# A fused attention and two-MLP kernel: the weights' buffers move 32 bytes within SBUF, the moving sides stay

## The chip, the core and the metric

The kernel runs on one core of one Trainium2 chip. The metric is the device time of one execution in microseconds (us); lower is better. A core has TensorE (PE; its weight loads are listed apart as PEld), VectorE (DVE), ScalarE (ACT), GpSimd (POOL) and SyncE (SP, which issues the DMAs here). SBUF is the on-chip memory of 128 partitions; a tile occupies the same bytes in each of them, so one byte address per partition says where a tile lies.

## The reference

Causal attention with 2 batches, 12 heads, 448 positions and head size 64 gives 896 tokens of 768 values. Two dense layers follow:

```python
x = attn_out.transpose(0, 2, 1, 3).reshape(B * S, H * D)   # 896 x 768
h = (x @ w1) * (x @ w2) @ w3                               # 768 -> 1024 -> 1024
x = h @ w_out                                              # 1024 -> 768
h = x @ w_in                                               # 768 -> 2048
g = h * np.clip(h + 3.0, 0.0, 6.0) / 6.0
out = g @ w_out2                                           # 2048 -> 768
```

## The kernel before

**Arithmetic.** Every dense product is made from two float32r parts of each operand, a high one and a low one, with three matmuls: high times high, high times low, low times high (the three `nc.tensor.matmul` in the `go` functions). Each matmul has its own load of 128 x 128 weights (LDWEIGHTS) and a moving side of 448 columns (one batch), or 384 columns for the product of weights.

**Stages.** Attention runs first (scores `s` L469, transposes `ptp` L517, values `o` L542), and beside it and after it the product of two weight matrices, `w_out` and `w3` (`pw`, L614). Then come the products with `w1` and `w2` (`pa`, L747), with the product of weights (`px`, L863), and with `w_in` and `w_out2` (`pg`, L747, and `po`, L928). `pa` and `pg` use seven products in place of eight (the function `multiply`; `side` names the seven). `Plan.issue` decides the order of all instructions on each engine beforehand, by ranks and by costs written as constants; no address enters it.

**Where the operands lie.** Pools are laid out one after the other. From low addresses: 1,152 bytes of other things, `consts` (pool `cp`), then pool `ws` with seven buffers of 8,192 bytes: three `raw` (where weights land from HBM: `vir`, `vor`, `w1r`, `wrr`, `wpr`, `w3r`) and four `hl` (the high and low parts that TensorE loads as weights: `w3`, `w2a` to `w2d`, `wp`, `vja`, `vjb`, `vo`). Then the empty tile `gap`, and pool `xp` with the attention output `xt`, later `x2t`. Further up lie `wr` (moving side of `pw`), `ab` and `g` (moving sides of `px` and `po`), and the tiles T1 to T4 (moving sides of `pa` and `pg`).

All steps inside these tiles from one operand of a matmul to the next (from the high part to the low one, from one block of 128 rows to the next, from batch to batch) are multiples of 256 bytes, as are the distances between buffers of one pool, modulo 256. So every dense matmul has one place modulo 256 bytes for its weights and one for its moving side. In the built program, before:

- `hl` weights start at 160 modulo 256 (25,760 is the first).
- Moving sides (`xt`, `x2t`, `T1` to `T4`, `wr`, `ab`, `g`) start at 224 modulo 256.
- Three of the seven products of `pg` (P6, P3 and P4 of `multiply`) take their weights from `xp` tiles (named `v` in the profile), from element 16 on (`ASIDE`, L46): 32 modulo 256.

Below, *the distance* is the start of the moving side minus the start of the weights, modulo 256: 64 for all `hl` weights, 192 for the weights `v`. Of the 2,256 dense matmuls, 384 (`pw`), 576 (`po`), 288 (`px`), 576 (`pa`) and 216 of the 432 of `pg` take `hl` weights; the other 216 take `v`.

The lines that hold these places:

```python
            s2, a22, s4 = ((own(i), ASIDE) for i in range(3))        # pg: weights in xp tiles
            s2, a22 = ((parts(f"{f[0]}{c}", f[1]), 0) for c in "cd") # pa: weights in hl buffers
```

Of the kernel before, what the change touches and what calls it, by code (L numbers as in the profile page):

```python
# [9 lines left out]
F32 = mybir.dt.float32  # L10
# [178 lines left out]
def attention_moe_moe2(ctx: ExitStack, tc, q, k, v, w1, w2, w3, w_out, v_in, v_out, out):  # L189
# [12 lines left out]
    P = 128  # L202
# [22 lines left out]
    cp = ctx.enter_context(tc.tile_pool(name="cp", bufs=1))  # L225
    ws = ctx.enter_context(tc.tile_pool(name="ws", bufs=2))

    gap = ctx.enter_context(tc.tile_pool(name="gap", bufs=1))
    gap.tile([P, 16], F32, name="gap")
    xp = ctx.enter_context(tc.tile_pool(name="xp", bufs=1))  # L230

    dp = ctx.enter_context(tc.tile_pool(name="dp", bufs=1, space=bass.MemoryType.DRAM))
    pd = ctx.enter_context(tc.tile_pool(name="pd", bufs=DENSE_BANKS, space=PSUM))
    consts = cp.tile([P, 8], F32, name="consts")
    three = consts[:, :1]

    ctx.enter_context(tc.manual_schedule())
# [769 lines left out]
```

## Time and profile before

| | before |
|---|---|
| time, median of 3 runs (lowest to highest) | 546.82 us (546.42 to 547.03) |
| time of the profiled execution | 546.7 us |
| its span, first to last instruction | 544.9 us |
| TensorE busy with matmuls | 538.9 us of 544.9 |
| VectorE, ScalarE, GpSimd busy | 72%, 55%, 21% of the span |
| granted TensorE clock, mean | 0.999 |

The span is what the trace covers; 1.8 us of the time lie around it. Busy time of TensorE counts each matmul from its start to its modelled end, and matmuls overlap; how fast TensorE goes is therefore read from the starts of matmuls that follow each other.

### The profile page before, as it was taken

What the parts mean: (1) busy time and instruction counts of PE and PEld (TensorE: products, weight loads), DVE (VectorE), ACT (ScalarE), POOL (GpSimd) and SP (SyncE); (2) the same over time, 40 slices, a digit from 0 to 9 for tenths busy, and PEclk for the clock granted to TensorE, in tenths of its full rate; (3) what the DMA queues carried; (4) which work ended last, traced back from release to release, by engine and by line L of the source; (5) the groups of instructions that cost most, each with busy time, mean ns of one, the idle gap of its engine ahead of it and who ended that gap; (6) DMA issues with size and microseconds to landing.
All of it is one profiled execution on the core that took longest, in us unless ns stands there. A gap on an engine that the chain in (4) does not pass through costs nothing.

```text
span 544.9 us, 8101 instructions
## 1 busy us (share of the span) xinstructions
PE 538.9 (99%) x2886; PEld 485.0 (89%) x2886; DVE 394.8 (72%) x746; ACT 298.2 (55%) x582; POOL 114.7 (21%) x150
## 2 busy tenths in 40 slices
PE   9999999999999999999999999999999999999997
PEld 7767677789999999999999999998999999999996
DVE  4888878777924798988728659998977876776322
ACT  4778777776525465544525336986656642653000
POOL 4778568571001111110000111010110101000000
PEclk9999999999999999999999999999999999999999
DMA  8687676436143333322513012538284647563664
GB/s 318 234 292 252 221 264 214 165 111 202 44 117 130 117 115 117 117 96 97 213 59 115 1 58 90 182 152 293 86 305 159 242 130 252 182 230 101 196 194 135
DMA packets 33224, 89.91 MB, mean 165 GB/s; under 512 B 3232, under 2 KB 21664, under 8 KB 30624
## 3 DMA queue, kind: packets, MB, share of 16 engines
q1 hardware_dynamic: 33184, 89.40, 48.2%
q8 instruction: 22, 0.36, 0.3%
q14 instruction: 18, 0.15, 0.1%
HBM read 75.24 MB, written 14.16 MB: 164 GB/s over the span
## 4 chain that ended last, share of the span: by engine, by line
PE 97%; DMA 1%; ACT 0%; DVE 0%; issue 0%; POOL 0%; SPq 0%; POOLq 0%; ACTq 0%
PE po L928 21%; PE pw L614 12%; PE paX L747 11%; PE px L863 11%; PE pgX L747 10%; PE s L469 7%; PE paZ L747 5%; PE pgZ L747 5%; PE o L542 5%; PE ptp L517 4%; PE paY L747 3%; PE pgY L747 2%; DMA vir<-in_moe_w_in 1%; PE warm L570 1%; PE warm L448 1%; DVE wr L305 0%
## 5 line engine op out<-in xcount | busy, mean ns | idle before, releaser
L928 PE MATMUL po<-g,vo 128*128 128x448 f32 x576 | 116.3, 362 | 0.0
L928 PEld LDWEIGHTS po<-g,vo 128*128 128x128 f32 x576 | 108.0, 187 | 7.2
L614 PE MATMUL pw<-wr,w 128*128 128x384 f32 x384 | 75.9, 347 | 0.3 <-DVE wr L305 0.3
L495 POOL TENSOR_SCALAR prb<-prb,sums 128x448 f32<-128x448 f32 (+6 forms) x84 | 65.5, 796 | 32.9 <-DVE sums L489 16.8
L614 PEld LDWEIGHTS pw<-wr,w 128*128 128x128 f32 x384 | 65.8, 188 | 2.2 <-issue 0.7
L863 PE MATMUL px<-ab,wp 128*128 128x448 f32 x288 | 57.9, 362 | 0.0
L863 PEld LDWEIGHTS px<-ab,wp 128*128 128x128 f32 x288 | 54.0, 187 | 3.6
L715 DVE TENSOR_TENSOR o<-po,o 128x448 f32<-128x448 f32 x36 | 22.4, 623 | 38.6 <-PE po L928 36.7
L469 PE MATMUL s<-ks,qs 128*128 128x448 f32 (+6 forms) x168 | 48.1, 392 | 0.0
L472 DVE CUSTOM_DVE_ANT_0 z<-s,maskb 128x448 f32<-128x448 f32 (+6 forms) x84 | 34.4, 420 | 18.4 <-PE s L469 9.4
L476 ACT ACTIVATE prb<-z,sums 128x448 f32<-128x448 f32 (+6 forms) x84 | 42.3, 508 | 4.7 <-DVE sums L472 4.7
L299 POOL TENSOR_SCALAR vja<-vir 128x768 fp32r<-128x768 f32 x8 | 7.6, 946 | 172.9 <-DVE x2t L697 70.4
L469 PEld LDWEIGHTS s<-ks,qs 128*128 128x128 f32 x168 | 27.3, 190 | 6.1 <-issue 0.9
L525 ACT COPY pt<-ptp 128x512 f32<-128x512 f32 (+1 forms) x48 | 24.8, 561 | 11.9 <-PE ptp L517 11.8
L517 PEld LDWEIGHTS ptp<-ident,prb 128*128 128x128 f32 x192 | 22.2, 139 | 5.7 <-issue 3.1
L542 PE MATMUL o<-pt,vr 128*64 128x448 f32 (+3 forms) x192 | 25.8, 393 | 0.0
L303 ACT CAST vo<-vor 128x1024 fp32r<-128x1024 f32 x12 | 13.6, 1132 | 21.6 <-PE po L928 18.1
L517 PE MATMUL ptp<-ident,prb 128*128 128x128 f32 x192 | 25.4, 272 | 0.0
L542 PEld LDWEIGHTS o<-pt,vr 128*64 128x64 f32 (+1 forms) x192 | 11.3, 135 | 15.2 <-issue 10.0
L708 DVE SCALAR_TENSOR_TENSOR g<-rab,g 128x448 fp32r<-128x448 f32 x32 | 20.6, 651 | 1.1 <-ACT g L706 1.1
L706 ACT ACTIVATE g<-rab 128x448 fp32r<-128x448 f32 x32 | 18.3, 578 | 4.7 <-DVE rab L704 4.7
L702 ACT ACTIVATE rab<-q,consts 128x448 f32<-128x448 f32 x24 | 16.0, 669 | 8.5 <-DVE q L892 8.1
(148 smaller groups left out, 1051.9 us busy)
## 6 DMA issues: line engine op xcount, KB each, us to landing
vor<-in_moe_w_out SPq DMA_DIRECT2D x12, 1024.0 KB, 6.5
w3r<-in_moe_w SPq DMA_DIRECT2D x8, 1024.0 KB, 5.1
sums_of<-o SPq DMA_DIRECT2D x36, 224.0 KB, 2.7
o<-sums_of SPq DMA_DIRECT2D x36, 224.0 KB, 2.7
wrr<-in_moe_w_out SPq DMA_DIRECT2D x8, 768.0 KB, 6.3
w1r<-in_moe_w SPq DMA_DIRECT2D x8, 768.0 KB, 5.4
w2r<-in_moe_w SPq DMA_DIRECT2D x8, 768.0 KB, 4.3
vjr<-in_moe_w_in SPq DMA_DIRECT2D x8, 768.0 KB, 4.7
```

The lines of the kernel that those rows point to most:

```text
L469: plan.op("pe", pe4(n), lambda: nc.tensor.matmul(ps[:, :n], qs[u][:, t].rearrange("p h i -> p (h i)"), ks[u][:, :n], start=True, stop=True ...
L472: plan.op("dve", dve(n) + 0.09, lambda: nc.vector.tensor_tensor_reduce(out=z[:, :n], in0=ps[:, :n], in1=maskb[:, S - n:], scale=-SCALE, sc ...
L476: plan.op("act", act(n, True) + 0.2, lambda: nc.scalar.activation(pb[:, OFF[t]:OFF[t] + n], z[:, :n], AF.Exp, bias=sm[:, 0, t:t + 1], scal ...
L495: nc.gpsimd.tensor_scalar(s, s, sm[:, 1, t:t + 1], 1.0, ALU.mult, ALU.mult)
L517: nc.tensor.transpose(ps[:w, i * P:(i + 1) * P], pb[:, OFF[t] + kb * P:OFF[t] + kb * P + w], ident)
L525: plan.op("act", act(cut), lambda: nc.scalar.copy(dst()[:, :cut], ps[:, :cut]), reads=[ps], writes=[d.at((g, 0))], rank=rank)
L542: nc.tensor.matmul(ps[T * j:T * j + T, kb * P:S], vr[u][:w, kb, j, :], d[:w, base[kb]:base[kb] + TQ - 2 * kb, j, :], start=kb == 0, stop=k ...
L614: nc.tensor.matmul(ps[:, :W], weight(n, a, kk), hls[m][:, c, at_:at_ + W], start=kk == 0 and a == c, stop=kk == KF - 1 and a == LO)
L715: plan.op("dve", dve(S), lambda: nc.vector.tensor_tensor(o[:, :], ps[:, :S], o[:, :], ALU.add), reads=[ps], writes=[o], rank=rank)
L747: nc.tensor.matmul(ps[:, :S], hl[:, a, off + kk * P:off + (kk + 1) * P], t[:, c], start=first and kk == 0 and a == c, stop=kk == HK - 1 an ...
L863: nc.tensor.matmul(ps[m, b][:, :S], weight(n, a, kk), ab[kk][:, c, cols(b)], start=kk == 0 and a == c, stop=kk == KF - 1 and a == LO)
L928: nc.tensor.matmul(ps[:, :S], hls[n][:, a, at_:at_ + P], gt[k][:, d, cols(b)], start=kk == 0 and a == d, stop=kk == KC - 1 and a == LO)
```

## The change

`consts` grows from 32 to 64 bytes and `gap` shrinks from 64 to 32. So the seven buffers of `ws` lie 32 bytes higher (1,184 becomes 1,216 for the first, 25,760 becomes 25,792 for the first `hl`), and every tile from `xp` on stays where it was (`xp` begins at 58,592 in both). `hl` weights now start at 192 modulo 256, and their distance to every moving side is 32 where it was 64. The weights `v` stay at distance 192. The instructions and their order are the same on all five engines; only addresses in `ws` differ.

```diff
     ws = ctx.enter_context(tc.tile_pool(name="ws", bufs=2))
 
     gap = ctx.enter_context(tc.tile_pool(name="gap", bufs=1))
-    gap.tile([P, 16], F32, name="gap")
+    gap.tile([P, 8], F32, name="gap")
     xp = ctx.enter_context(tc.tile_pool(name="xp", bufs=1))
...
-    consts = cp.tile([P, 8], F32, name="consts")
+    consts = cp.tile([P, 16], F32, name="consts")
     three = consts[:, :1]
```

## Rows read from the trace of the kernel before

**Rows 1.** The page, part 1: busy time, share and instructions by engine.
```profile
PE 538.9 (99%) x2886; PEld 485.0 (89%) x2886; DVE 394.8 (72%) x746; ACT 298.2 (55%) x582; POOL 114.7 (21%) x150
```
**Rows 2.** All waits of TensorE: total, times, longest in us.
```profile
PE warm L448 <- POOL ident masks.py:199: 1.4, 1, 1.4
PE pgZ L747 <- ACT q L889: 0.6, 1, 0.6
PE pw L614 <- DVE wr L305: 0.3, 1, 0.3
```
**Rows 3.** The chain that ended last: start, length in us, instructions in a row.
```profile
13.08 2.62 PE warm L570 x24
...
127.24 38.17 PE pw L614 x219
...
266.81 57.00 PE px L863 x285
```
**Rows 4.** The same chain over one part of `pg` and around it.
```profile
404.07 1.80 PE pgX L747 x9
405.87 1.81 PE pgY L747 x9
407.67 1.81 PE pgX L747 x9
409.49 1.80 PE pgZ L747 x9
411.29 1.80 PE pgX L747 x9
413.09 1.82 PE pgZ L747 x9
414.91 1.81 PE pgX L747 x9
416.73 9.60 PE po L928 x48
```
**Rows 5.** Timeline of TensorE there: start, length, operands; weights are the second name.
```profile
403.91 1.96 PE L747 MATMUL pgX<-x2t,vja 128*128 128x448 f32 x9
405.71 1.97 PE L747 MATMUL pgY<-x2t,vja 128*128 128x448 f32 x9
407.51 1.98 PE L747 MATMUL pgX<-T2g,v 128*128 128x448 f32 x9
409.33 1.96 PE L747 MATMUL pgZ<-T1g,vjb 128*128 128x448 f32 x9
411.13 1.97 PE L747 MATMUL pgX<-T3g,vjb 128*128 128x448 f32 x9
412.93 1.98 PE L747 MATMUL pgZ<-x2t,v 128*128 128x448 f32 x9
414.75 1.98 PE L747 MATMUL pgX<-T4g,v 128*128 128x448 f32 x9
416.57 0.96 PE L928 MATMUL po<-g,vo 128*128 128x448 f32 x4
```
**Rows 6.** Busy time by stretch: length, each engine's busy us (instructions), clock, DMA share, GB/s.
```profile
127.00:167.00 40.00, 40.00 (x232) 39.84 (x233) 25.07 (x39) 19.37 (x35) 3.15 (x3) 1.00 0.34 105
267.00:324.00 57.00, 57.00 (x287) 53.43 (x286) 32.80 (x50) 21.78 (x35) 2.42 (x3) 1.00 0.20 65
324.00:362.00 38.00, 38.00 (x191) 35.45 (x190) 35.83 (x57) 29.78 (x51) 4.09 (x5) 1.00 0.40 146
362.00:493.00 131.00, 130.45 (x651) 121.67 (x651) 105.18 (x155) 76.73 (x117) 9.41 (x9) 1.00 0.58 197
```
**Rows 7.** The chain around TensorE's one wait for data in `pg`.
```profile
372.45 7.04 DMA vir<-in_moe_w_in
...
379.57 0.93 ACT vir L323
380.50 0.42 ACT q L889
...
380.96 2.08 PE pgZ L747 x9
```

## The prediction, made before the changed kernel ran

> **What bounds the kernel now.** I read the busy shares first, then TensorE's waits, then the chain that ended last with the count of matmuls in each of its pieces. TensorE is busy 538.9 of 544.9 us [rows 1], and all its waits for other engines come to 1.4 + 0.6 + 0.3 = 2.3 us [rows 2]. So the time is the sum of the intervals between the starts of matmuls, and only what changes such an interval, or makes a wait longer, can change the time. The granted clock is 1.00 in the stretches shown, its 2.4 GHz level [rows 6].
>
> The interval itself: 285 matmuls of `px` in 57.00 us are 200.0 ns each, and 219 of `pw` in 38.17 us are 174.3 [rows 3]. `px` streams 448 columns, `pw` 384. At one column per clock these would be 186.7 and 160.0 ns, so each interval has some 13 to 14 ns on top, about the same for both lengths. It does not grow with the columns, so it goes with something that happens once in a matmul, and what does is the load of the next weights. That load runs while the matmul streams: two streams read SBUF at once, and the change shifts one against the other.
>
> Does their relative place cost anything? One part of `pg` has both sorts of weights side by side. With `hl` weights (distance 64) nine matmuls take 1.80 us from the first start to the next nine's: 403.91 to 405.71, 405.71 to 407.51, 409.33 to 411.13, 411.13 to 412.93. With the weights `v` (distance 192) they take 1.82: 407.51 to 409.33, 412.93 to 414.75, 414.75 to 416.57 [rows 5]. The chain gives the price with fewer rounding errors: from 404.07 to 416.73 us are 63 matmuls in 12.66 us [rows 4]; 36 of them at 200.0 ns are 7.20, which leaves 5.46 us for the 27 with `v`, 202.2 ns each. The pairs differ in nothing else that I find: same shape, same type, same tile T or `x2t` as moving side. So the distance, or the place of the weights, is worth 2.2 ns a matmul between 64 and 192. This is the one row on which the forecast rests.
>
> **The change part by part.** *Constants and gap.* Nothing is computed with the added bytes; 0 us. *The `raw` buffers.* DMAs write them 32 bytes higher, and ACT, DVE and POOL read them there. The trace has no transfer or instruction at another place, so nothing prices this directly. Below, a gain is bounded by the only wait that such work ends: 0.6 us before `pgZ`, behind a load of 7.04 us [rows 2, 7]. Above, VectorE in 324 to 362 us is busy 35.83 of 38.00 [rows 6]: it could slow by 2.17 us, 6%, before it fills this stretch. I take 0 for both, since TensorE is what covers them (busy 38.00 of 38.00 there), and keep a rival for the end above.
>
> *The `hl` weights.* The distance goes from 64 to 32 for 384 + 576 + 288 + 576 + 216 = 2,040 matmuls, 1,656 of them with 448 columns. The 216 with `v` stay as they are. No dense matmul of before has the distance 32; the nearest rows are 64 (200.0 ns) and 192 (202.2). From below: if 64 isn't the cheapest distance, I can bound the gain only by the whole excess, 13.3 ns x 2,040 = 27 us; a gain of the size of the one difference that the trace shows is 2.2 x 1,656 = 3.6 us. From above: one more excess of the same size, 13.3 x 2,040 = 27 us. There is also a row at distance 0, but in plain float32: the 24 `warm` transposes of 128 columns take `ident` for both sides, and 109 ns each [rows 3] are 0.85 ns a column, half the speed of `px`, with only 2.5 ns left over two clocks a column. At half the speed two streams in one place disturb each other little; at full speed no row tells.
>
> I take the price of the row with `v`, that is +2.2 ns, on the matmuls of 448 columns: 1,656 x 2.2 ns = 3.6 us. Why this and not 0: the interval demonstrably depends on where the two streams start, and a distance of 32 puts the weights' first reads nearer to the moving side's than in either row, so that keeping the cheaper of the two prices would be the luckier result. For `pw` (384 columns; no row at another distance) the bounds are 0 and 384 x 2.2 = 0.8 us; I take half, 0.4. Sum: 3.6 + 0.4 = +4.0 us on the profiled execution's 546.7, 550.7 us. That execution lies 0.1 us below the median of the runs, 546.82, so that the two bases agree.
>
> **The rivals.**
>
> *No change.* The two streams run at different speeds (weight loads are busy 53.43 of 57.00 us of `px` for 128 columns each, against 448 that move [rows 6]), so they drift past each other, and a shift of 32 bytes moves the meetings without changing their number; or weights and moving side don't meet at all, and the 13 ns belong to the swap of weights. For it: the excess is about the same in `pw` and `px` [rows 3], and the `warm` row shows two streams from one address at little cost. Against it: 202.2 beside 200.0 [rows 4]. Then every interval stays, 546.8 us. The Trainium skill, TensorE: Matmul & The Clock Gate, section Step-by-step: what each phase is for, states this as a rule: TensorE has two independent SBUF read ports, and loading the next weights doesn't steal read bandwidth from the running matmul. The Trainium skill, SBUF — State Buffer, section SBUF: two separate sides, agrees: only VectorE and GpSimd share a port. By that rule, address differences cost nothing and the time stays; the trace doesn't settle it, but 1.82 beside 1.80 us [rows 5] speaks against its strict form.
>
> *Faster.* 64 is not the cheapest distance, or a start of the weights at 192 modulo 256, a multiple of 64, lets a load touch one unit less than a start at 160 or 32, which are both 32 beyond such a multiple. For it: each start in the trace, of `hl`, of `v` and of the moving sides, is 32 beyond a multiple of 64, so no row excludes it. Against it: the one other distance is dearer. Sized by the same 2.2 ns, 1,656 + half of 384 matmuls give -4.0 us: 542.7 us.
>
> *A real collision.* With the streams 32 bytes apart the moving side stands still for about as long again as it does now: +13.3 ns x 2,040 = 27 us, 574 us; half of it gives 560. This decides from about +6 ns a matmul on. Against it: nothing in dense rows; the `warm` row shows none at half speed.
>
> *VectorE fills its stretch.* If reads and writes in the shifted buffers cost VectorE over 6% more, 324 to 362 us is bound by it: above 548 us. The trace shows nothing that would slow it.
>
> **How the numbers follow.** The forecast, +1.1 to +7 us, has 0.40; no change 0.29; faster 0.22; a collision of 7 us and more 0.08; VectorE 0.01. A difference of 0.2%, 1.1 us, is about what a measurement of this kernel can tell from no change. So slower has 0.49, same 0.29, faster 0.22. The range reaches down to a gain of 1.2 times the one sized above (542 us, some 0.08 below it) and up into the collision case (557 us, +4.6 ns a matmul, some 0.08 above it). The likeliest case alone spans 548 to 554 us.
>
> **What would show it.** The chain's piece of 285 `px` matmuls is the cleanest gauge: 57.0 us means no change, 57.6 the forecast (202.2 ns each), 56.4 the faster rival, above 58.5 a collision. The pieces with `v` should stay at 1.82 us in all cases; if they move too, the distance isn't what counts. `pw`'s 219 should go from 38.2 to between 38.2 and 38.7. VectorE's means should stay. The forecast is wrong if 32 bytes are below the grain at which the streams meet, or if the dearer price of `v` comes from where its high and low parts lie and not from the distance.

## The result and the profile after

The changed kernel takes 552.49 us in the median of 4 runs (552.24 to 553.25), beside 546.62 for the kernel before: a ratio of 1.0102, 95% interval 1.0083 to 1.0121. It is slower: the medians differ by 5.87 us, the spans of the two profiles (550.5 and 544.9 us) by 5.6. The profiled execution took 552.24 us.

One number from ahead of the prediction has to be put right first: `pa` and `pg` have 504 matmuls each, not 576 and 432, and of those of `pg` 288 take `hl` weights. The sums that the prediction uses (2,040 matmuls with `hl` weights, 1,656 of them with 448 columns, 216 with `v`) stand.

The page's busy times and all waits of TensorE, after (compare [rows 1, 2]):

```profile
PE 545.0 (99%) x2886; PEld 486.4 (88%) x2886; DVE 394.7 (72%) x746; ACT 298.9 (54%) x582; POOL 115.2 (21%) x150
```
```profile
PE warm L448 <- POOL ident masks.py:199: 1.4, 1, 1.4
PE pw L614 <- DVE wr L305: 0.3, 1, 0.3
```

TensorE is busy 6.1 us longer; VectorE, ScalarE and GpSimd are busy as long as before within 0.7 us. No wait came in, and the one of 0.6 us in `pg` is gone. So the loss is in the intervals of TensorE itself. The chain that ended last, after (start, length, instructions in a row; compare [rows 3]), and behind it the pieces of before that [rows 3] does not show:

```profile
128.22 38.16 PE pw L614 x219
...
271.15 58.90 PE px L863 x285
...
498.64 48.02 PE po L928 x240
```
```profile
165.41 1.80 PE paX L747 x9
...
323.81 1.80 PE pgX L747 x9
...
493.11 48.02 PE po L928 x240
```

`pw` with its 384 columns is as before (38.17). `px` takes 58.90 us for 285, 206.7 ns each, in place of 57.00, 200.0 ns each. But `po` takes 48.02 us for 240, 200.1 ns each, as before, with the same new distance of 32. So the distance alone doesn't set the interval. The place where it falls, in the chain of after at the start of `pg`:

```profile
330.05 1.86 PE pgX L747 x9
331.91 1.85 PE pgY L747 x9
333.76 1.21 PE pgX L747 x6
334.97 1.80 PE pgZ L747 x9
336.77 2.41 PE pgX L747 x12
...
341.58 1.82 PE pgZ L747 x9
```

And the timeline there, which names the weights:

```profile
329.88 2.02 PE L747 MATMUL pgX<-x2t,vja 128*128 128x448 f32 x9
331.75 2.02 PE L747 MATMUL pgY<-x2t,vja 128*128 128x448 f32 x9
333.60 1.37 PE L747 MATMUL pgX<-T2g,v 128*128 128x448 f32 x6
334.81 1.96 PE L747 MATMUL pgZ<-T1g,vjb 128*128 128x448 f32 x9
336.61 1.36 PE L747 MATMUL pgX<-x2t,vja 128*128 128x448 f32 x6
```

Twice nine matmuls with `vja` take 1.86 and 1.85 us (206 or 207 ns each by their starts, but for the last) up to the first piece with weights `v`, six matmuls at 333.6 us. Right behind these six, nine with `vjb`, whose distance is the same as that of `vja`, take 1.80 us, and no stretch with `hl` weights goes back to 1.86 for the rest of the kernel. From the end of `pw` (128.22 + 38.16 = 166.38, before 165.41) to the first matmul of `pg` (330.05, before 323.81) the changed kernel loses 163.67 - 158.40 = 5.27 us; 792 matmuls there at 6.67 ns each would be 5.28. Behind that, up to the last 240 of `po`, it is 0.71 us shorter than before (168.59 beside 169.30): the 18 slow matmuls at the start of `pg` cost 0.12 us, and the wait of 0.6 us is gone. The rest of the span's difference, 0.98 us ahead of `pw`, is scatter between executions as far as the profiles show: the six whose operands lie up to there as after the change start `pw`'s 219 anywhere from 127.52 to 128.62 us, and that of before with `ASIDE` 48 (below), whose `hl` weights lie as before, starts them at 128.46, beside 127.24.

The theory made of this, *the rhythm*: at distance 32 a row of matmuls can go on in either of two rhythms, 200.0 or 206.7 ns, and keeps the one that it is in. What came before decides; here the hand-over from `pw` brings the slow one, and the first weights at distance 192 end it. Its rivals: the operands of `pa` and `px` cost 206.7 ns and those of `pg` and `po` don't (*the stage*); or it is the place of the weights alone, a multiple of 64, and not the distance (*the place*).

### The profile page after: what moved, and what is told of

It is laid out like the page before. It is cut to its first block, busy times and chain, and to the rows that moved or that the text cites. A ratio compares the mean times of both kernels' runs of the same rounds, so it can differ in the third digit from the quotient of the medians.

```text
span 550.5 us, 8101 instructions
## 1 busy us (share of the span) xinstructions
PE 545.0 (99%) x2886; PEld 486.4 (88%) x2886; DVE 394.7 (72%) x746; ACT 298.9 (54%) x582; POOL 115.2 (21%) x150
## 4 chain that ended last, share of the span: by engine, by line
PE 99%; DVE 0%; issue 0%; POOL 0%; POOLq 0%
PE po L928 21%; PE pw L614 12%; PE px L863 11%; PE paX L747 11%; PE pgX L747 11%; PE s L469 7%; PE paZ L747 5%; PE pgZ L747 5%; PE o L542 5%; PE ptp L517 4%; PE paY L747 3%; PE pgY L747 3%; PE warm L570 1%; PE warm L448 1%; DVE wr L305 0%
## 5 line engine op out<-in xcount | busy, mean ns | idle before, releaser
L863 PE MATMUL px<-ab,wp 128*128 128x448 f32 x288 | 59.8, 369 | 0.0
L299 POOL TENSOR_SCALAR vja<-vir 128x768 fp32r<-128x768 f32 x8 | 9.0, 1122 | 174.7 <-PE px L863 72.9
```

What stands on the lines that cost most here:

```text
L863: nc.tensor.matmul(ps[m, b][:, :S], weight(n, a, kk), ab[kk][:, c, cols(b)], start=kk == 0 and a == c, stop=kk == KF - 1 and a == LO)
```

## Experiments

Ratios are to the kernel before in the same rounds, each with its 95% interval.

**All dense operands 32 bytes higher, distance 64.** The changed kernel with `gap` back at 64 bytes; a pad of 224 bytes moves T1 to T4 to the same place.

```diff
-    gap.tile([P, 8], F32, name="gap")
+    gap.tile([P, 16], F32, name="gap")
...
-        ph.close()
+        ph.close(); right.enter_context(tc.tile_pool(name="pad", bufs=1, side="right")).tile([P, 56], F32, name="pad")
```

> The changed kernel with all dense operands moved up by 32 bytes: weights start at 192 modulo 256 as after the change, moving sides at 0, so that the distance is 64 again. Theory 'relative place': the time goes back to before, 546.8 us, the 285 matmuls of px take 57.0 us. Rival 'place of the weights alone' (192 is a bad start): 552.4 us and 58.9 us for px.

547.21 us, ratio 1.000 (0.9987 to 1.0013). The chain of this run:

```profile
267.16 57.00 PE px L863 x285
...
493.74 48.02 PE po L928 x240
```

The weights start at 192 here as after the change, and cost nothing. The place of the weights alone falls as a cause.

**Distance 32 at another place.** `consts` of 96 bytes, `gap` of 32 and the same pad: the weights start at 224 modulo 256, the moving sides at 0.

```diff
-    consts = cp.tile([P, 16], F32, name="consts")
+    consts = cp.tile([P, 24], F32, name="consts")
```

> The changed kernel with weights and moving sides all 32 bytes higher: distance 32 as after the change, but the weights start at 224 modulo 256, 32 beyond a multiple of 64 like before, and the moving sides at 0. If the distance alone decides: px 58.9 us for 285 and 552.4 us. If it takes weights that start at a multiple of 64 (192): px 57.0 us and 546.8 us.

552.60 us, ratio 1.0104 (1.0077 to 1.0132), with both rhythms in the same stages as after the change:

```profile
270.78 58.90 PE px L863 x285
...
500.28 48.02 PE po L928 x240
```

With the run before, this shows that the distance matters and not where both lie.

**Three matmuls added at distance 192, and a control.** The changed kernel; the three go ahead of the second product of `pa`, and what they write is overwritten. In the control the slice begins at 0, distance 32.

```diff
             def go(kk=kk, t=t):
+                if kind == "w2" and f == 0 and name == "P2" and kk == 0:
+                    for _ in range(3):
+                        nc.tensor.matmul(ps[:, :S], hl[:, HI, 24:24 + P], t[:, HI], start=True, stop=False,
+                                         skip_group_check=True)
```

> The changed kernel with three matmuls added at the start of the second product of pa, whose weights start 96 bytes further (distance 192); their result is overwritten. Theory 'rhythm' (at distance 32 a row of matmuls keeps either 200.0 or 206.7 ns, whichever it is in, and a few at distance 192 set it to 200.0): pa after the three and all of px run at 200.0 ns, px 57.0 us for 285; 552.4 - 0.0067 x 800 + 0.6 = 547.6 us. Rival 'stage' (pa and px cost 206.7 ns because of their operands): 552.4 + 0.6 = 553.0 us, px 58.9 us.

> The control: the same three added matmuls with their weights at distance 32. Both theories: pa and px stay at 206.7 ns, px 58.9 us, 552.4 + 0.6 = 553.0 us. If px falls to 57.0 us here too, it is an interruption of the pattern of three, and not the distance 192, that sets the rhythm.

553.08 us, ratio 1.0111 (1.0091 to 1.0131), and 552.87 us, 1.0108 (1.0093 to 1.0123). The three at distance 192 took 0.61 us and changed nothing right behind them; the chain around them:

```profile
166.20 1.85 PE paX L751 x9
168.04 0.61 PE paY L748 x3
168.65 1.86 PE paY L751 x9
170.51 1.86 PE paX L751 x9
```

This is a miss for the rhythm as I had put it: a few matmuls at distance 192 don't end it. In `pg` it was six, in the order of a product (high times high, high times low, low times high), where these three are all high times high. The next run tries nine in that order; its expectation speaks of nine in `pg` too, but the timeline above shows six.

**A whole product added at distance 192, and its control.** Nine matmuls in the order of a product, with high and low parts; in the control the slices begin at `i * P`, distance 32.

```diff
+                if kind == "w2" and f == 0 and name == "P2" and kk == 0:
+                    for i in range(3):
+                        for a, c in ((HI, HI), (HI, LO), (LO, HI)):
+                            nc.tensor.matmul(ps[:, :S], hl[:, a, i * P + 24:i * P + 24 + P], t[:, c],
+                                             start=i == 0 and a == c, stop=False, skip_group_check=True)
```

> The changed kernel with nine matmuls added at the start of pa's second product, in the order of a whole product of pg (high-high, high-low, low-high for three blocks), weights 96 bytes further, so at distance 192; their result is overwritten. In pg nine such matmuls end the slow rhythm, in the run with three added they did not. Theory 'rhythm, and the whole pattern at distance 192 ends it': pa and px at 200.0 ns from there, px 57.0 us for 285, 552.4 - 5.3 + 1.8 = 548.9 us. Rival 'what ends it in pg is not the distance but something else at that place': px stays at 58.9 us, 554.2 us.

> The control of the run with nine added matmuls: the same nine with their weights at distance 32. If distance 192 ends the slow rhythm: px stays at 58.9 us, 552.4 + 1.9 = 554.3 us. If any nine that break the order do: px 57.0 us, 549 us.

With distance 192: 549.45 us, ratio 1.0037 (1.0024 to 1.0050). The control: 554.32 us, 1.0134 (1.0112 to 1.0155). The chain of the former around the nine (L749), and its `px`:

```profile
166.78 1.85 PE paX L752 x9
168.62 1.81 PE paY L749 x9
170.44 1.80 PE paY L752 x9
172.24 1.80 PE paX L752 x9
...
270.04 57.00 PE px L868 x285
```

And the control's:

```profile
165.74 1.85 PE paX L752 x9
167.59 1.86 PE paY L749 x9
169.45 1.86 PE paY L752 x9
...
272.37 58.90 PE px L868 x285
```

Work of 1.8 us added makes the changed kernel some 3 us faster. Every matmul of `pa` and `px` behind the nine has the same operands, addresses and order as in the control and runs at 200.0 ns instead of 206.7. The stage falls as the cause; the rhythm stands, and here a whole product at distance 192 ended the slow one.

It doesn't always do that. In the run with three added at distance 192, TensorE waits 0.96 us in `pg` for ScalarE, ahead of the nine matmuls with `v` in the first line; up to the wait `pg` was in the fast rhythm. The chain from there:

```profile
414.58 2.08 PE pgX L751 x9
416.67 1.86 PE pgZ L751 x9
418.53 1.85 PE pgX L751 x9
420.38 1.82 PE pgZ L751 x9
```

The two products behind these nine, with `hl` weights at distance 32, are in the slow rhythm again, until the next product with `v` ends it. A wait of 0.9 us at the same place in the run with distance 32 at another place, and one of 0.5 us in the control with nine, were not followed by it. So what a product at distance 192 hands over depends on something more, which no run isolates.

**Nothing left at distance 192.** The changed kernel with the weights `v` moved within their tiles to distance 32.

```diff
-ASIDE = 16
+ASIDE = 56
```

> The changed kernel with ASIDE 56 in place of 16, so that the weights v lie at distance 32 like all others. Theory 'rhythm': nothing at distance 192 is left that could set the rhythm back, so pg and po stay at 206.7 ns too: 552.4 + (216 + 576) x 0.0067 + 216 x 0.0045 = 558.7 us, po's last 240 in 49.6 us. Rival 'stage' (pg and po cost 200.0 ns at distance 32 anyway): v falls from 202.2 to 200.0 ns, 552.4 - 0.5 = 551.9 us, po's last 240 in 48.0 us.

558.18 us, ratio 1.0187 (1.0146 to 1.0229). Now the slow rhythm lasts to the end:

```profile
270.96 58.90 PE px L863 x285
...
503.46 49.61 PE po L928 x240
```

`po` at distance 32 costs 206.7 ns when nothing has ended the rhythm, where it cost 200.1 after the change. Of the four runs one took 553.73 us and three 557.77 to 558.66; two rhythms that a chance can choose between would do that, but the run of 553.73 has no trace, so this isn't shown.

**The weights `v` at distance 64.** The kernel before with `ASIDE` 48.

```diff
-ASIDE = 16
+ASIDE = 48
```

> The kernel before with ASIDE 48 in place of 16: the weights v lie in the same tiles as before, at distance 64 like all others. If the distance sets the interval, their nine matmuls take 1.80 us in place of 1.82, the time is 546.7 - 0.5 = 546.2 us. If the tile or the place of its high and low parts does, they stay at 1.82 us and 546.7.

546.56 us, beside 547.27 for the kernel before in the same rounds: ratio 0.9985 (0.9976 to 0.9995). Its chain, over one part of `pg` behind a wait (the last two before `po`, from 413.80 and 415.60 us on, have weights `v`; compare the 1.82 and 1.81 of [rows 4]):

```profile
412.00 1.80 PE pgX L747 x9
413.80 1.80 PE pgZ L747 x9
415.60 1.80 PE pgX L747 x9
```

So the 2.2 ns of `v` belong to the distance and not to the tile. This is the one version that is faster than both kernels; below the kernel before it is by a small 0.15%, and its interval ends 0.05% short of no difference.

**Other distances.** The kernel before with the weights 64 bytes higher (distance 0), 32 lower (96), and, with pads for T1 to T4, distances 128 and 192; `v` stays at 192. For 0 and 96 the edits are:

```diff
-    gap.tile([P, 16], F32, name="gap")
...
-    consts = cp.tile([P, 8], F32, name="consts")
+    consts = cp.tile([P, 24], F32, name="consts")
```
```diff
-    gap.tile([P, 16], F32, name="gap")
+    consts = gap.tile([P, 24], F32, name="consts")
...
-    consts = cp.tile([P, 8], F32, name="consts")
```

The one for 128 is that for 96 with 32 elements in place of 24 and a pad of 56; the one for 192 makes `gap` 48 elements, with a pad of 32.

> The kernel before with the weights' buffers 32 bytes lower and all else in place (consts lies in the gap): distance 96. If only nearness hurts, 200.0 ns each, 546.7 us. If every start of the weights that is a multiple of 64 or 128 allows the slow rhythm (weights at 128 modulo 256 here), some stretches at 206.7 ns, 549 to 559 us.

> The kernel before with the weights' buffers 64 bytes higher: weights and moving sides start at the same place, distance 0. If the price grows with nearness: over 206.7 ns each, 546.7 + 1,656 x 6.7 ns or more = over 558 us. If distance only shifts the pattern by which the streams meet: between 200 and 206.7 ns, 546 to 558 us.

> The kernel before with all dense operands at distance 192, where before only v lies. If the row on which the prediction rested is the settled price of that distance, all 1,872 matmuls of 448 columns that are at 200.0 ns before (1,656 and, unchanged at 202.2, the 216 of v) take 202.2 ns: px 57.6 us, 546.7 + 1,656 x 2.2 ns = 550.4 us. If 202.2 is only the price of going over from one distance to another and back, px is 57.0 us or falls into 206.7 ns, 58.9 us.

> The kernel before with distance 128 for all but v. If the price repeats every 128 bytes, it is that of distance 0, which had 206.7 ns in pa and px and 202.7 in po: px 58.9 us and about 554 us. If it repeats every 256 bytes or not at all, another time; below 200.0 ns each it would be a faster kernel than both.

The chains, in the order of distance 0, 96, 128 and 192:

```profile
271.14 58.90 PE px L863 x285
...
500.21 48.66 PE po L928 x240
```
```profile
128.64 38.89 PE pw L614 x219
...
271.62 58.52 PE px L863 x285
...
502.42 49.30 PE po L928 x240
```
```profile
127.81 38.74 PE pw L614 x219
...
269.97 58.14 PE px L863 x285
...
499.47 48.97 PE po L928 x240
```
```profile
127.72 38.16 PE pw L614 x219
...
268.41 57.63 PE px L863 x285
...
496.70 48.55 PE po L928 x240
```

Each length by its count, with the two kernels of the study:

| distance | ns each in `px` | in `po` | time, us | ratio |
|---|---|---|---|---|
| 0 | 206.7 | 202.8 | 554.23 | 1.0135 (1.0120 to 1.0150) |
| 32 (after) | 206.7 | 200.1 | 552.49 | 1.0102 (1.0083 to 1.0121) |
| 64 (before) | 200.0 | 200.1 | 546.62 | |
| 96 | 205.3 | 205.4 | 556.22 | 1.0172 (1.0157 to 1.0187) |
| 128 | 204.0 | 204.0 | 554.27 | 1.0133 (1.0111 to 1.0154) |
| 192 | 202.2 | 202.3 | 551.11 | 1.0077 (1.0049 to 1.0104) |

Distance 0 has two prices by stage, as 32 has. 96, 128 and 192 have one each. The price doesn't grow with nearness: 96 costs more time in all than 0. Nor does it repeat every 128 bytes: 64 and 192 differ, and so do 0 and 128. The 202.2 ns at distance 192 is a settled price, as [rows 4] said; 200.0 at 64 is the lowest of the six.

But it is a mean, and few single matmuls have it. By the starts in the traces, two of three intervals at 192 are 199 to 201 ns and the third is 206 or 207, with `v` before as in `px` here; at 128 the intervals of `px` are 212, 200, 209, 196 and 203 ns, over and over. In the slow rhythm at 32 every one is 206 or 207 ns, in `po` after the change every one is 200. So each price belongs to a pattern over several matmuls and not to one matmul.

## Why the prediction came out right, and where its reasoning did not

**The bound.** Right: no wait came in, other engines kept their busy times, and the time moved by what the intervals of TensorE did.

**The relative place of the two streams costs time.** Right, and shown: distance 64 elsewhere in SBUF has the time of before, distance 32 elsewhere that of after. The step weighed a row, 1.82 beside 1.80 us, against the rule of the Trainium skill, TensorE: Matmul & The Clock Gate, section Step-by-step: what each phase is for, that loading the next weights doesn't steal read bandwidth from the running matmul. By that rule the time would have stayed; the measurements differ, with 200.0 to 206.7 ns for the same matmuls at six distances. Whether it is the two reads that get in each other's way, no run shows.

**The price at distance 32.** This is the step that failed: "I take the price of the row with `v`, that is +2.2 ns, on the matmuls of 448 columns: 1,656 x 2.2 ns = 3.6 us." The price is right at its own distance: with all `hl` weights at 192, `px` takes 202.2 ns each, and the 551.11 us are near the 550.4 that this price gives. Taking it over to 32 had no row behind it, and there is no one price at 32. Some 800 matmuls, in `pa`, in `px` and in the first two products of `pg`, paid 6.7 ns more, and the others nothing. 5.4 us came of it, not far from 3.6, because a price three times as high fell on half as many. The forecast of 550.7 beside 552.49 is good by that coincidence and not by its sum. The gauge that I named told it: `px` at 58.9 us was above the 58.5 that the text assigns to a collision, not at the 57.6 of the forecast, while `po` was at the value for no change.

**`pw`.** Taken at +0.4 us from the price at 192; 38.16 us for 219 beside 38.17, so nothing, and nothing at 192 either (38.16). A price read on 448 columns doesn't hold for 384.

**Constants, `raw` buffers, VectorE.** 0 us taken, and nothing is seen there. The pieces with `v` stayed at 1.82 us, as forecast for all cases.

**The rivals.** *No change* holds for `pw`, `po` and most of `pg` alone. *Faster* through a start at a multiple of 64 is excluded by the run with everything 32 bytes higher: 192 as a start at distance 64 brought nothing; and none of the other five distances that ran is cheaper than 64 (160 and 224 did not run). *A real collision* had the right size in `pa` and `px`, but its reason, nearness, falls with the row for distance 96. (The upper end of the forecast's range, 557 us, is 5.0 ns on each of the 2,040 matmuls, not the 4.6 given there.) The remark that keeping the cheaper price at 32 "would be the luckier result" holds in an unforeseen way: it depends on what ran before.

**Open:** why there are two rhythms, why `pa` starts in the slow one behind `pw`, and which property of the nine matmuls, and of the six in `pg`, ends it (the three were all high parts, the others had the full order, so both number and order differ), and why nine behind a wait once brought it back. No run separates these. Nor does any run show what the 13 ns over one column per clock are that remain at distance 64.

## What to carry to other kernels

Where TensorE is busy throughout and loads new weights for each matmul, the byte distance between weights and moving side is a knob worth some 1 to 2% here: measure the interval over a long row of equal matmuls (length by count in the chain) at several distances, for every pair of buffers that meets, because neither nearness nor a period of 128 bytes orders the six here. Don't multiply a price read at one place by the count of matmuls elsewhere before you have seen it in each stage: the same pair of addresses can run at two rates, and what ran before has a part in which.

## What the runs showed of the hardware that I had not expected

A row of equal matmuls can keep one of two intervals, 200.0 or 206.7 ns at distance 32, over hundreds of matmuls and three kinds of product, while the mean granted clock is 0.998 to 1.000 in all runs. A whole product of nine at distance 192 moved it from the slow one to the fast one; three matmuls at that distance, or nine at distance 32, didn't. Once, behind a wait of 0.96 us, nine at distance 192 were followed by the slow one. And at most distances the price is the mean of a repeating pattern of unequal intervals: 197 to 202 ns in `px` at 64, 196 to 212 at 128.
